# A Fourier mixing layer and a SoLU block: up projection by even and odd parts for tokens k and -k

## The chip, the cores and the metric

The program runs on one core of one Trainium2 chip. The core has five engines that run side by side, each through a queue of its own in order: TensorE (PE, with its weight loads PEld) multiplies matrices into PSUM, VectorE (DVE) and ScalarE (ACT) work on PSUM and SBUF, GpSimd (POOL) works on SBUF, and SyncE (SP) issues transfers; ACT and POOL issue transfers too. The metric is the device time of one execution in microseconds, as the median of several runs.

## The reference

The input x has 8 batches of 3136 tokens with 256 features. A 2D Fourier transform over tokens and features is taken and its real part kept; each of the 25088 tokens then goes through an up projection, a SoLU, a layer norm and a down projection.

```python
X = np.fft.fft(x, axis=1)
X = np.fft.fft(X, axis=2)
x = X.real.reshape(B * S, D)
h = x @ w_in                                   # 256 -> 1024
e = np.exp(h - np.max(h, axis=-1, keepdims=True))
solu = h * e / (np.sum(e, axis=-1, keepdims=True) + 1e-09)
mu = np.mean(solu, axis=-1, keepdims=True)
var = np.mean((solu - mu) ** 2, axis=-1, keepdims=True)
out = (solu - mu) / np.sqrt(var + 1e-06) * g_ln @ w_out   # 1024 -> 256
```

## The kernel before

Everything is float32. A matmul of this type is two instructions in the trace.

**The transform.** A token index is n = 64 n1 + n2, a frequency k = k1 + 49 k2. Batches are taken in 4 pairs. For a pair, x is folded with its mirror x[-n, -d] (`fold`, lines 116 to 128: two sums on POOL, then even and odd parts in the features on DVE), summed over n1 on TensorE (`transform1`, 16 calls a pair, each copied from PSUM by ACT), written to a scratch in HBM and read back with n2 on the partitions (`turn`, 4 transfers on SP). `transform2` then makes, for one k1 of 0 to 24, the 128 tokens of both batches (64 k2 each), as 256 folded features: the cosine part at 0 to 128, the sine part at 129 to 255. The feature transform is folded into w_in before the loop (`Wi`), so that h is the folded features times `Wi`. Token -k has the same cosine part and the sine part negated.

**Two token tiles from one transform2.** DVE copies the PSUM tile to `q` for tokens k (line 169). For tokens -k two ACT steps write `qm`, in reversed order of k2 and with the sine features negated (line 176). From then on k and -k are two separate tiles of 128 tokens: 196 tiles, `+` and `-` in turn (k1 = 0 has no `-`).

**The second part, for one tile.** `up_half` multiplies `q` or `qm` with one half of `Wi` (two calls for the two halves of the features, added in PSUM). `solu`: DVE takes the negated row maximum of h (line 195), ACT the exponential with its sum (198), DVE the product u = h e with its sum (200), POOL the negated mean (203), ACT the centred square with its sum (206), POOL the scale `rs` by four small steps (209 to 215). `transpose` turns u on TensorE in two halves of four; ACT copies the first half to `uT`, DVE the second. `down` is 8 calls with `Wo`, then DVE scales the result into `ot` (237), and SP stores it by two transfers of 64 rows (240).

**The order of the work** is written out by hand (lines 364 to 382) and is the order on every engine: for tile i and the tile before it, the first half of up of i, transposes of i - 1, the second half of up of i, solu of i; after a `+` tile, transform2 for the next k1 and one step of the next pair's sequence transform (`ahead`, 25 steps: loads, 4 folds, 16 transform1, turn); then down of i - 1.

**Buffers that matter.** PSUM has 8 banks: two h tiles of two banks (`ps_h`), two of `tp` (`ps_t`) and two of tag `m` (`ps_m`). The `m` buffers are taken in turn by transform2, transform1 and down. The loads of x use two buffers for each of `xa` and `xb`; xb, the mirrored rows, come by an indirect gather that POOL issues, with row numbers from `idx`.

Before the loop the weights, which come as 64-bit floats, are narrowed on DVE, `Wi` and `Wo` are prepared, and the first pair is transformed.

Of the kernel before, what the change touches and what calls it, by code (L numbers as in the profile page):

```python
# [10 lines left out]
I32 = mybir.dt.int32  # L11
# [6 lines left out]
# The sequence index is n = N2 * n1 + n2 and its frequency k = k1 + N1 * k2.  # L18
# The frequencies k1 of 0..NK-1 are computed; k1 and N1 - k1 share their products.
# [8 lines left out]
# The layout of the 256 folded features: cosine part at 0..128, sine part (1..127) at 129..255.  # L28
# [4 lines left out]
def kernel(  # L33
# [38 lines left out]
    ps_h = ctx.enter_context(tc.tile_pool(name="ps_h", bufs=2, space=PSUM))  # L72
# [9 lines left out]
    neg_half = const.tile([P, 1], FP32, name="neg_half")  # L82
    idx = const.tile([PR, NP * NC], I32, name="idx")
    sg = const.tile([P, 1], FP32, name="sg")

# [8 lines left out]
    def load(pr, c):  # L94
        """Rows n2 = 8c + 1 .. 8c + 8, and those of S - n beside them (in descending order of n2)."""
        r = slice(pr.p * PR, (pr.p + 1) * PR)
        xa = xpool.tile([PR, CH, D], FP32, tag="xa", name="xa")
        xb = xpool.tile([PR, CH, D], FP32, tag="xb", name="xb")
        nc.sync.dma_start(out=xa, in_=x_pn[r, c * CH + 1 : (c + 1) * CH + 1, :])
        i = pr.p * NC + c  # L100
        nc.gpsimd.indirect_dma_start(
            out=xb.rearrange("p l d -> p (l d)"), out_offset=None, in_=x_g,
            in_offset=bass.IndirectOffsetOnAxis(ap=idx[:, i : i + 1], axis=0))
# [12 lines left out]
    def fold(pr, c):  # L116
        """x[n, d] + x[-n, -d], then its even and odd parts in d. Rows n2 = 0 and 32 hold their own mirrors."""
        xa, xb, x0 = pr.raw.pop(c)
# [3 lines left out]
        nc.gpsimd.tensor_tensor(out=a[:, :, 0:1], in0=a[:, :, 0:1], in1=rb[:, :, 0:1], op=ALU.add)  # L122
        y = xpool.tile([PR, CH, D], FP32, tag="y", name="y")
# [31 lines left out]
    def turn(pr):  # L155
        """(b, cosine or sine, n2) onto partitions."""
# [5 lines left out]
    def transform2(pr, k1):  # L162
        """Sum over n2 for both batches; out: folded features on partitions, tokens (b, k2) free."""
        ps = ps_m.tile([P, KD, P], FP32, tag="m", name="ps2")
        for h in range(KD):
            nc.tensor.matmul(ps[:, h, :], pr.g[:, k1, h * P : (h + 1) * P], T[:, k1, :],  # L166
                             start=(h == 0), stop=(h == KD - 1), skip_group_check=True)
        q = {"+": qpool.tile([P, KD, P], FP32, tag="q", name="q")}
        nc.vector.tensor_copy(out=q["+"], in_=ps)  # L169
        if k1:  # L170
            # -(k1 + 49 k2) is (49 - k1) + 49 (63 - k2): the negative frequencies run backwards.
            q["-"] = qpool.tile([P, KD, P], FP32, tag="qm", name="qm")
            for h in range(KD):
                o = q["-"][:, h, :].rearrange("p (b k) -> p b k", b=2)
                i = ps[:, h, :].rearrange("p (b k) -> p b k", b=2)[:, :, ::-1]
                nc.scalar.activation(out=o, in_=i, func=ACT.Copy, scale=sg if h else 1.0)  # L176
        return q

# [1 line left out]

    class Tokens:
        def __init__(self, p, k1, s):
            self.p, self.k1, self.s = p, k1, s

    def up_half(t, half):
        if half == 0:
            t.h = ps_h.tile([P, FF], FP32, tag="h", name="h")
        fs = slice(half * HW, (half + 1) * HW)
        for h in range(KD):
            nc.tensor.matmul(t.h[:, fs], t.q[:, h, :], Wi[:, h, fs], start=(h == 0), stop=(h == KD - 1))  # L190

    def solu(t):
        """u = h exp(h - max h), its sum and centred sum of squares, and the sum of the exponentials."""
        nmax = small.tile([P, 1], FP32, tag="nmax", name="nmax")
        nc.vector.tensor_reduce(out=nmax, in_=t.h, axis=AX.X, op=ALU.max, negate=True)  # L195
        t.u = fpool.tile([P, FF], FP32, tag="u", name="u")
        esum = small.tile([P, 1], FP32, tag="esum", name="esum")
        nc.scalar.activation(out=t.u, in_=t.h, func=ACT.Exp, bias=nmax, accum_out=esum)  # L198
        usum = small.tile([P, 1], FP32, tag="usum", name="usum")
        nc.vector.scalar_tensor_tensor(out=t.u, in0=t.h, scalar=1.0, in1=t.u, op0=ALU.mult, op1=ALU.mult,  # L200
                                       accum_out=usum)
        nmean = small.tile([P, 1], FP32, tag="nmean", name="nmean")
        nc.gpsimd.tensor_scalar(out=nmean, in0=usum, scalar1=-1.0 / FF, scalar2=None, op0=ALU.mult)  # L203
        sq = fpool.tile([P, FF], FP32, tag="sq", name="sq", bufs=1)
        ssq = small.tile([P, 1], FP32, tag="ssq", name="ssq")
        nc.scalar.activation(out=sq, in_=t.u, func=ACT.Square, bias=nmean, accum_out=ssq)  # L206
        # 1 / (sum * sqrt(var(u / sum) + 1e-6)) = (var(u) + 1e-6 sum^2) ** -0.5
        es = small.tile([P, 1], FP32, tag="es", name="es")
        nc.gpsimd.tensor_scalar(out=es, in0=esum, scalar1=1e-9, scalar2=1e-3, op0=ALU.add, op1=ALU.mult)
        es2 = small.tile([P, 1], FP32, tag="es2", name="es2")  # L210
        nc.gpsimd.tensor_tensor(out=es2, in0=es, in1=es, op=ALU.mult)
        v = small.tile([P, 1], FP32, tag="v", name="v")
        nc.gpsimd.tensor_scalar(out=v, in0=ssq, scalar1=1.0 / FF, scalar2=es2, op0=ALU.mult, op1=ALU.add)  # L213
        t.rs = small.tile([P, 1], FP32, tag="rs", name="rs")
        nc.gpsimd.tensor_tensor(out=t.rs, in0=v, in1=neg_half, op=ALU.pow)  # L215

    def transpose(t):
        t.uT = fpool.tile([P, KF, P], FP32, tag="uT", name="uT")
        n = KF // 2
        for half in range(2):  # L220
            tp = ps_t.tile([P, n, P], FP32, tag="t", name="tp")
            for c in range(n):
                f = half * n + c
                nc.tensor.matmul(tp[:, c, :], t.u[:, f * P : (f + 1) * P], ident, is_transpose=True,  # L224
                                 start=(c == 0), stop=(c == n - 1), skip_group_check=True)
            o = t.uT[:, half * n : (half + 1) * n, :]
            if half:
                nc.vector.tensor_copy(out=o, in_=tp)  # L228
            else:
                nc.scalar.copy(o, tp)  # L230

    def down(t):
        ps = ps_m.tile([P, D], FP32, tag="m", name="ps_o")
        for c in range(KF):
            nc.tensor.matmul(ps, t.uT[:, c, :], Wo[:, c, :], start=(c == 0), stop=(c == KF - 1))  # L235
        ot = fpool.tile([P, D], FP32, tag="ot", name="ot", bufs=3)
        nc.vector.tensor_scalar(out=ot, in0=ps, scalar1=t.rs, scalar2=None, op0=ALU.mult)  # L237
        for b in range(2):
            ob = out_b[2 * t.p + b].rearrange("(k2 k1) d -> k1 k2 d", k1=N1)
            nc.sync.dma_start(out=ob[t.k1 if t.s == "+" else N1 - t.k1], in_=ot[b * N2 : (b + 1) * N2, :])  # L240

# [1 line left out]

    def load_weight(pool, w, o, engine):
        """o = w in float32 (rows split as "(c p)"). A float64 w comes as its bits, in words of 32."""
# [11 lines left out]
        def narrow(c, j):  # L257
# [4 lines left out]
            # The exponent, from a bias of 1023 to one of 127.  # L262
# [5 lines left out]
            # top: sign, exponent and the 20 mantissa bits of the high word; unit: the same with no mantissa.  # L268
# [6 lines left out]
            # The low word as a number, by halves that float32 holds exactly.  # L275
# [16 lines left out]
    def load_weights(pool):  # L292
        w_in = pool.tile([P, KD, FF], FP32, name="w_in")
        g_ln = pool.tile([P, KF], FP32, name="g_ln")
        Q = pool.tile([P, KD, D], FP32, name="Q")
# [3 lines left out]
        nc.scalar.dma_start(out=sg, in_=sign)  # L299
# [5 lines left out]
        def prepare():  # L305
            narrow_in()
            for h in range(KD):
                ps = ps_h.tile([P, FF], FP32, tag="h", name="wps")
                for half in range(2):
                    fs = slice(half * HW, (half + 1) * HW)  # L310
                    for c in range(KD):
                        nc.tensor.matmul(ps[:, fs], Q[:, c, h * P : (h + 1) * P], w_in[:, c, fs],
                                         start=(c == 0), stop=(c == KD - 1))
# [137 lines left out]
```

## Time and profile before

| what | us |
| --- | --- |
| median of 3 runs (2170.12 to 2171.92) | 2170.22 |
| span of the profiled execution (first to last instruction) | 2166.9 |
| PE busy in it, 6992 matmul instructions | 1788.7 |
| DVE busy | 846.8 |
| ACT busy | 670.6 |
| POOL busy | 382.0 |

One page sums the whole execution: busy time, share of the span and number of instructions of each engine. Other views cut it: windows give the busy time of each engine in a stretch, with the clock that TensorE was granted (1.00 is full speed) and the DMA share; waits say which engine and line waited for which, with the total, the number of times and the longest; groups (`line engine op out<-in shapes xcount | busy, mean ns | idle before`) give a mean duration; a timeline gives start, duration, engine, line and step, with the idle time before it and what ended that in brackets. PE and PEld durations of neighbouring instructions overlap, so the price of a TensorE step is read from start to start. The loop over the tiles begins at 136.6 us.

### The profile page before, as it was taken

What the parts mean: (1) busy time and instruction counts of PE and PEld (TensorE: products, weight loads), DVE (VectorE), ACT (ScalarE), POOL (GpSimd) and SP (SyncE); (2) the same over time, 40 slices, a digit from 0 to 9 for tenths busy, and PEclk for the clock granted to TensorE, in tenths of its full rate; (3) what the DMA queues carried; (4) which work ended last, traced back from release to release, by engine and by line L of the source; (5) the groups of instructions that cost most, each with busy time, mean ns of one, the idle gap of its engine ahead of it and who ended that gap; (6) DMA issues with size and microseconds to landing.
All of it is one profiled execution on the core that took longest, in us unless ns stands there. A gap on an engine that the chain in (4) does not pass through costs nothing. (4 is left out here: it accounts for less than half of the span.)

```text
span 2166.9 us, 19414 instructions
## 1 busy us (share of the span) xinstructions
PE 1788.7 (83%) x6992; PEld 1238.2 (57%) x6992; DVE 846.8 (39%) x1327; ACT 670.6 (31%) x1240; POOL 382.0 (18%) x1034
## 2 busy tenths in 40 slices
PE   2357888788799878878879987887887999999998
PEld 1135555555566555555556755555555666777666
DVE  2853233323334323332433433333233344444444
ACT  1113223223333322332332323233233234434443
POOL 3002121212112212121211221212121111111111
PEclk8679899889899888888999988889899899999999
DMA  9511010001042101000104210101010400000000
GB/s 240 133 33 42 24 46 13 25 13 28 10 90 75 42 20 50 12 26 12 28 11 88 77 42 16 54 10 28 11 29 11 88 18 18 17 16 18 18 18 17
DMA packets 56783, 84.78 MB, mean 39 GB/s; under 512 B 12038, under 2 KB 50574, under 8 KB 51696
## 3 DMA queue, kind: packets, MB, share of 16 engines
q1 hardware_dynamic: 48528, 65.19, 12.7%
q0 software_dynamic: 2048, 12.85, 2.1%
q10 hardware_dynamic: 6112, 5.52, 1.3%
q8 instruction: 55, 0.90, 0.2%
q14 instruction: 40, 0.33, 0.1%
HBM read 44.72 MB, written 38.80 MB: 39 GB/s over the span
## 5 line engine op out<-in xcount | busy, mean ns | idle before, releaser
L235 PE MATMUL ps_o<-Wo,uT 128*128 128x256 f32 x3136 | 833.5, 425 | 270.8 <-ACT qm L176 215.9
L235 PEld LDWEIGHTS ps_o<-Wo,uT 128*128 128x128 f32 x3136 | 668.7, 217 | 444.7 <-ACT qm L176 235.5
L198 ACT ACTIVATE u<-h,nmax 128x1024 f32<-128x1024 f32 x196 | 218.4, 1114 | 634.3 <-DVE nmax L195 634.3
L190 PE MATMUL h<-Wi,q 128*128 128x512 f32 x800 | 384.4, 604 | 7.8 <-DVE q L169 7.8
L190 PE MATMUL h<-Wi,qm 128*128 128x512 f32 x768 | 361.1, 592 | 0.0
L200 DVE SCALAR_TENSOR_TENSOR u<-h,u 128x1024 f32<-128x1024 f32 x196 | 240.0, 1225 | 249.4 <-ACT u L198 249.4
L206 ACT ACTIVATE sq<-u,nmean 128x1024 f32<-128x1024 f32 x196 | 225.1, 1148 | 317.7 <-POOL nmean L203 317.7
L195 DVE TENSOR_REDUCE nmax<-h 128x1 f32<-128x1024 f32 x196 | 239.9, 1224 | 193.5 <-PE h L190 193.5
L203 POOL TENSOR_SCALAR nmean<-usum 128x1 f32<-128x1 f32 x196 | 45.7, 233 | 1515.3 <-DVE u L200 1515.3
L228 DVE COPY uT<-tp 128x512 f32<-128x512 f32 x196 | 135.5, 691 | 372.3 <-PE tp L224 372.3
L230 ACT COPY uT<-tp 128x512 f32<-128x512 f32 x196 | 114.9, 586 | 415.9 <-PE tp L224 415.9
L224 PEld LDWEIGHTS tp<-ident,u 128*128 128x128 f32 x1568 | 183.5, 141 | 104.5 <-issue 103.7
L237 DVE TENSOR_SCALAR ot<-ps_o,rs 128x256 f32<-128x256 f32 x196 | 94.0, 480 | 369.4 <-issue 364.3
L190 PEld LDWEIGHTS h<-Wi,q 128*128 128x128 f32 x800 | 147.5, 195 | 115.4 <-issue 103.7
L224 PE MATMUL tp<-ident,u 128*128 128x128 f32 x1568 | 203.2, 273 | 0.5 <-DVE u L200 0.5
L190 PEld LDWEIGHTS h<-Wi,qm 128*128 128x128 f32 x768 | 138.4, 190 | 96.8 <-issue 91.8
L215 POOL TENSOR_TENSOR rs<-v,neg_half 128x1 f32<-128x1 f32 x196 | 113.2, 578 | 16.3
L148 PE MATMUL ps<-y,F 98*100 98x258 f32 (+3 forms) x288 | 71.5, 385 | 43.3 <-DVE y L114 43.3
L166 PEld LDWEIGHTS ps<-T,g 128*128 128x128 f32 x400 | 60.4, 191 | 47.4 <-issue 47.4
L213 POOL TENSOR_SCALAR v<-ssq,es 128x1 f32<-128x1 f32 x196 | 52.4, 267 | 177.6 <-ACT sq L206 175.5
L148 PEld LDWEIGHTS ps<-y,F 98*100 98x100 f32 x288 | 45.5, 178 | 54.7 <-DVE y L114 30.4
L121 POOL TENSOR_TENSOR xa<-xa,xb 98x2040 f32<-98x2040 f32 (+1 forms) x16 | 70.1, 4379 | 28.9 <-DMA xa<-in_x_dram 16.2
(50 smaller groups left out, 544.4 us busy)
## 6 DMA issues: line engine op xcount, KB each, us to landing
out_dram<-ot SPq DMA_DIRECT2D x392, 64.0 KB
zd<-z SPq DMA_DIRECT2D x16, 800.0 KB
g<-zd SPq DMA_DIRECT2D x16, 800.0 KB
xa<-in_x_dram SPq DMA_DIRECT2D x16, 784.0 KB
raw_in_moe_w_in_dram<-in_moe_w_in_dram ACTq DMA_DIRECT2D x1, 2048.0 KB
raw_in_moe_w_out_dram<-in_moe_w_out_dram ACTq DMA_DIRECT2D x1, 2048.0 KB
T<-in_t_tab_dram ACTq DMA_DIRECT2D x2, 400.0 KB
x<-in_x_dram SPq DMA_DIRECT2D x4, 98.0 KB
```

The costliest lines, as they stand in the source:

```text
L148: nc.tensor.matmul(o[..., cs], F[:, 2 * t + h, :], i[..., cs], start=first, stop=True, skip_group_check=True)
L190: nc.tensor.matmul(t.h[:, fs], t.q[:, h, :], Wi[:, h, fs], start=(h == 0), stop=(h == KD - 1))
L195: nc.vector.tensor_reduce(out=nmax, in_=t.h, axis=AX.X, op=ALU.max, negate=True)
L198: nc.scalar.activation(out=t.u, in_=t.h, func=ACT.Exp, bias=nmax, accum_out=esum)
L200: nc.vector.scalar_tensor_tensor(out=t.u, in0=t.h, scalar=1.0, in1=t.u, op0=ALU.mult, op1=ALU.mult, accum_out=usum)
L206: nc.scalar.activation(out=sq, in_=t.u, func=ACT.Square, bias=nmean, accum_out=ssq)
L215: nc.gpsimd.tensor_tensor(out=t.rs, in0=v, in1=neg_half, op=ALU.pow)
L224: nc.tensor.matmul(tp[:, c, :], t.u[:, f * P : (f + 1) * P], ident, is_transpose=True, start=(c == 0), stop=(c == n - 1), skip_group_check ...
L228: nc.vector.tensor_copy(out=o, in_=tp)
L230: nc.scalar.copy(o, tp)
L235: nc.tensor.matmul(ps, t.uT[:, c, :], Wo[:, c, :], start=(c == 0), stop=(c == KF - 1))
L237: nc.vector.tensor_scalar(out=ot, in0=ps, scalar1=t.rs, scalar2=None, op0=ALU.mult)
```

## The change

Tokens k and -k of one k1 become one unit. Its up projection is made once for the cosine features (0 to 127, `up(t, 0)`) and once for the sine features (128 to 255, `up(t, 1)`) in two PSUM tiles. Feature 128, a cosine one, goes out of the second part: its column of `Wi` is kept apart as a row `w_mid`, the feature itself is brought onto token partitions by a further matmul with one column in transform2, and DVE adds it while it takes the even part from PSUM (`even`). DVE then makes h for k as even + odd and for -k as even - odd, with the row maximum in the same instruction (`join`); the maxima are negated by one small step. The `qm` copies go.

The tokens of -k are now in the order of k, so their rows in the output run backwards: they are stored by an indirect scatter that POOL issues (`idx` has a column for each). h now lies in SBUF; the square is written over it.

The order of steps is written anew for units, and the loop's fold is split: the sums on POOL (`add_mirror`) come one step before the DVE part (`fold`), and `ahead_pe` (transform1, turn) stands apart from `ahead` (load, add_mirror, fold). The four small steps for `rs` are made for both signs at once, in five.

```diff
-    ps_h = ctx.enter_context(tc.tile_pool(name="ps_h", bufs=2, space=PSUM))
+    ps_h = ctx.enter_context(tc.tile_pool(name="ps_h", bufs=1, space=PSUM))
...
-    idx = const.tile([PR, NP * NC], I32, name="idx")
-    sg = const.tile([P, 1], FP32, name="sg")
+    idx = const.tile([P, NP * (NC + NK - 1)], I32, name="idx")
+    w_mid = const.tile([P, FF], FP32, name="w_mid")
...
     def transform2(pr, k1):
-        ps = ps_m.tile([P, KD, P], FP32, tag="m", name="ps2")
+        ps = ps_m.tile([P, KD * P + 1], FP32, tag="m", name="ps2")
...
+        nc.tensor.matmul(ps[:, KD * P :], T[:, k1, :], pr.g[:, k1, P : P + 1],
+                         start=False, stop=True, skip_group_check=True)
+        return ps
+
+    def take2(ps):
+        q = qpool.tile([P, KD * P + 1], FP32, tag="q", name="q")
+        nc.vector.tensor_copy(out=q, in_=ps)
         return q
...
-    def up_half(t, half):
-        if half == 0:
-            t.h = ps_h.tile([P, FF], FP32, tag="h", name="h")
-        fs = slice(half * HW, (half + 1) * HW)
-        for h in range(KD):
-            nc.tensor.matmul(t.h[:, fs], t.q[:, h, :], Wi[:, h, fs], start=(h == 0), stop=(h == KD - 1))
+    def up(t, c):
+        ps = ps_h.tile([P, FF], FP32, tag=f"h{c}", name=f"ps_h{c}")
+        for half in range(2):
+            fs = slice(half * HW, (half + 1) * HW)
+            nc.tensor.matmul(ps[:, fs], t.q[:, c * P : (c + 1) * P], Wi[:, c, fs], start=True, stop=True)
+        return ps
+
+    def even(t, ps):
+        t.ev = fpool.tile([P, FF], FP32, tag="ev", name="ev", bufs=1)
+        nc.vector.scalar_tensor_tensor(out=t.ev, in0=w_mid, scalar=t.q[:, KD * P :], in1=ps,
+                                       op0=ALU.mult, op1=ALU.add)
+
+    def join(t, ps):
+        t.nmax = small.tile([P, 2], FP32, tag="nmax", name="nmax")
+        for s in t.signs:
+            t.h[s] = fpool.tile([P, FF], FP32, tag="h", name="h", bufs=2)
+            nc.vector.tensor_tensor_reduce(out=t.h[s], in0=t.ev, in1=ps, scale=1.0, scalar=-3.0e38,
+                                           op0=ALU.subtract if s else ALU.add, op1=ALU.max,
+                                           accum_out=t.nmax[:, s : s + 1])
+        n = len(t.signs)
+        t.neg = small.tile([P, 2], FP32, tag="neg", name="neg")
+        nc.vector.tensor_scalar(out=t.neg[:, 0:n], in0=t.nmax[:, 0:n], scalar1=-1.0, scalar2=None, op0=ALU.mult)
...
+    def store(t, s, ps):
+        ot = fpool.tile([P, D], FP32, tag="ot", name="ot", bufs=4)
+        nc.vector.tensor_scalar(out=ot, in0=ps, scalar1=t.rs[:, s : s + 1], scalar2=None, op0=ALU.mult)
+        if s:
+            i = NP * NC + t.p * (NK - 1) + t.k1 - 1
+            nc.gpsimd.indirect_dma_start(
+                out=out, out_offset=bass.IndirectOffsetOnAxis(ap=idx[:, i : i + 1], axis=0), in_=ot, in_offset=None)
+            return
...
+        if r == 4 and c + 1 < NC:
+            add_mirror(pr, c + 1)
         elif 0 <= c < NC and r == 0:
             fold(pr, c)
...
+            if cur:
+                even(cur, up(cur, 0))
+            if prv:
+                uT = transpose(prv, 0)
+            if cur:
+                odd = up(cur, 1)
+            if prv:
+                ps0 = down(prv, uT)
+            if cur:
+                join(cur, odd)
+                expo(cur)
+                product(cur, 0)
+            if prv:
+                store(prv, 0, ps0)
+            if two:
+                uT = transpose(prv, 1)
+            if nxt:
+                nxt.q = take2(transform2(pairs[nxt.p], nxt.k1))
+            if cur:
+                square(cur, 0)
+                if cur.p + 1 < NP:
+                    ahead_pe(pairs[cur.p + 1], cur.k1)
+            if two:
+                ps1 = down(prv, uT)
+            if cur:
+                if 1 in cur.signs:
+                    product(cur, 1)
+                    square(cur, 1)
+                stats(cur)
+                if cur.p + 1 < NP:
+                    ahead(pairs[cur.p + 1], cur.k1)
+            if two:
+                store(prv, 1, ps1)
```

`expo`, `product`, `square` and `stats` are the steps of `solu` for one sign (the last for both); `cur` is the unit at hand, `prv` the one before it, `nxt` the one after, and `two` says that `prv` has both signs. In the loop that prepares the weights a third product makes `w_mid`.

More of the change, by code (lines that the diff above doesn't have):

```diff
@@ new lines, in expo, with product @@
+    def expo(t):
+        t.esum = small.tile([P, 2], FP32, tag="esum", name="esum")
+        for s in t.signs:
+            t.u[s] = fpool.tile([P, FF], FP32, tag="u", name="u", bufs=4)
+            nc.scalar.activation(out=t.u[s], in_=t.h[s], func=ACT.Exp, bias=t.neg[:, s : s + 1],
+                                 accum_out=t.esum[:, s : s + 1])
+    def product(t, s):
+        if s == 0:
+            t.usum = small.tile([P, 2], FP32, tag="usum", name="usum")
+            t.nmean = small.tile([P, 2], FP32, tag="nmean", name="nmean")
+        nc.vector.scalar_tensor_tensor(out=t.u[s], in0=t.h[s], scalar=1.0, in1=t.u[s], op0=ALU.mult,
+                                       op1=ALU.mult, accum_out=t.usum[:, s : s + 1])
+        nc.gpsimd.tensor_scalar(out=t.nmean[:, s : s + 1], in0=t.usum[:, s : s + 1], scalar1=-1.0 / FF,
+                                scalar2=None, op0=ALU.mult)
@@ new lines, in square, with stats @@
+    def square(t, s):
+        if s == 0:
+            t.ssq = small.tile([P, 2], FP32, tag="ssq", name="ssq")
+        nc.scalar.activation(out=t.h[s], in_=t.u[s], func=ACT.Square, bias=t.nmean[:, s : s + 1],
+                             accum_out=t.ssq[:, s : s + 1])
+    def stats(t):
+        n = slice(0, len(t.signs))
+        es = small.tile([P, 2], FP32, tag="es", name="es")
+        nc.gpsimd.tensor_scalar(out=es[:, n], in0=t.esum[:, n], scalar1=1e-9, scalar2=1e-3,
+                                op0=ALU.add, op1=ALU.mult)
+        es2 = small.tile([P, 2], FP32, tag="es2", name="es2")
+        nc.gpsimd.tensor_tensor(out=es2[:, n], in0=es[:, n], in1=es[:, n], op=ALU.mult)
+        v = small.tile([P, 2], FP32, tag="v", name="v")
+        nc.gpsimd.tensor_scalar(out=v[:, n], in0=t.ssq[:, n], scalar1=1.0 / FF, scalar2=None, op0=ALU.mult)
+        nc.gpsimd.tensor_tensor(out=v[:, n], in0=v[:, n], in1=es2[:, n], op=ALU.add)
+        t.rs = small.tile([P, 2], FP32, tag="rs", name="rs")
+        nc.gpsimd.tensor_tensor(out=t.rs[:, n], in0=v[:, n], in1=neg_half[:, n], op=ALU.pow)
@@ L219, in transpose @@
+    def transpose(t, s):
+        uT = fpool.tile([P, KF, P], FP32, tag="uT", name="uT", bufs=2)
         n = KF // 2
@@ L367 @@
+        units[0].q = take2(transform2(pairs[0], 0))
+        for i in range(len(units) + 1):
+            cur = units[i] if i < len(units) else None
+            nxt = units[i + 1] if i + 1 < len(units) else None
+            prv = units[i - 1] if i else None
+            two = prv is not None and 1 in prv.signs
             if cur:
-                cur.q = qs[cur.p, cur.k1][cur.s]
-                up_half(cur, 0)
+                even(cur, up(cur, 0))
             if prv:
-                transpose(prv)
+                uT = transpose(prv, 0)
```

115 lines of the change are left out of this document (42 added, 73 removed).

## The prediction

> **What bounds the kernel now.** I read the busy time of the engines first, then windows over the span, then the waits.
>
> ```profile
> PE 1788.7 (83%) x6992; PEld 1238.2 (57%) x6992; DVE 846.8 (39%) x1327; ACT 670.6 (31%) x1240; POOL 382.0 (18%) x1034
> 900.00:1080.00 180.00, 144.06 (x544) 100.41 (x545) 62.20 (x93) 52.72 (x99) 30.72 (x79) 0.89 0.08 20
> 1900.00:2160.00 260.00, 258.63 (x1104) 181.81 (x1103) 120.77 (x179) 105.44 (x195) 48.30 (x165) 1.00 0.08 17
> PE ps_o L235 <- ACT qm L176: 215.9, 48, 4.5
> PE ps_o L235 <- DVE uT L228: 54.0, 12, 4.5
> ```
>
> In the windows (after the length: PE, PEld, DVE, ACT, POOL busy, then the clock) the last pair of batches keeps TensorE busy for 258.63 of 260 us at clock 1.00: TensorE bounds it. The earlier pairs also transform the next pair's sequence, and there TensorE is busy for 144 of 180 us at clock 0.89. The waits say why: 48 stalls behind `qm` (3 pairs x 16 calls of transform1) and 12 behind `uT` (3 x 4 folds), 4.5 us each. No other engine is busy for half the span.
>
> The timeline of the last pair gives the price of each step, from start to start:
>
> ```profile
> 1953.38 0.61 PE L166 MATMUL ps<-T,g 128*128 128x128 f32 x4
> 1953.82 3.62 PE L235 MATMUL ps_o<-Wo,uT 128*128 128x256 f32 x16
> 1957.22 0.42 DVE L169 COPY q<-ps 128x256 f32<-128x256 f32 x1
> 1957.28 1.88 PE L190 MATMUL h<-Wi,qm 128*128 128x512 f32 x4
> 1957.56 0.48 DVE L237 TENSOR_SCALAR ot<-ps_o,rs 128x256 f32<-128x256 f32 x1
> 1957.66 1.15 ACT L206 ACTIVATE sq<-u,nmean 128x1024 f32<-128x1024 f32 x1 [1.62 <-POOL nmean L203]
> 1958.99 1.04 PE L224 MATMUL tp<-ident,u 128*128 128x128 f32 x8
> 1959.63 0.59 ACT L230 COPY uT<-tp 128x512 f32<-128x512 f32 x1 [0.30 <-PE tp L224]
> 1959.87 1.88 PE L190 MATMUL h<-Wi,qm 128*128 128x512 f32 x4
> 1960.07 0.69 DVE L228 COPY uT<-tp 128x512 f32<-128x512 f32 x1 [2.03 <-PE tp L224]
> 1961.58 3.62 PE L235 MATMUL ps_o<-Wo,uT 128*128 128x256 f32 x16
> 1961.79 1.23 DVE L195 TENSOR_REDUCE nmax<-h 128x1 f32<-128x1024 f32 x1 [1.03 <-PE h L190]
> 1963.05 1.11 ACT L198 ACTIVATE u<-h,nmax 128x1024 f32<-128x1024 f32 x1 [2.83 <-DVE nmax L195]
> 1964.06 0.19 ACT L198 ACTIVATION_READ_ACCUMULATOR u<-h,nmax 128x1 f32 x1
> 1964.28 1.23 DVE L200 SCALAR_TENSOR_TENSOR u<-h,u 128x1024 f32<-128x1024 f32 x1 [1.27 <-ACT u L198]
> 1965.04 1.88 PE L190 MATMUL h<-Wi,q 128*128 128x512 f32 x4
> 1965.43 0.48 DVE L237 TENSOR_SCALAR ot<-ps_o,rs 128x256 f32<-128x256 f32 x1
> ```
>
> On TensorE: four up matmuls 1.71 (1957.28 to 1958.99), a transpose of eight 0.88, a down projection 3.46, transform2 0.44. A token tile is 2 x 1.71 + 0.88 + 3.46 = 7.76, a unit (k and -k) 15.96. Across engines: DVE sees a finished PSUM tile 0.21 after the next matmul begins (1961.58, 1961.79), a transposed half 0.2 after its matmuls; DVE to ACT takes 0.03; exp to product 1.23. Back to back, DVE begins the next step 0.08 before the last has ended (1957.22, 1957.56).
>
> **The stalls go.**
>
> ```profile
> 189.47 1.03 PE L148 MATMUL ps<-y,F 98*100 98x258 f32 x4
> 194.62 0.36 ACT L176 ACTIVATE qm<-ps,sg 128x128 f32<-128x128 f32 x1
> 195.03 5.41 PE L235 MATMUL ps_o<-Wo,uT 128*128 128x256 f32 x16 [4.53 <-ACT qm L176]
> 200.27 1.88 PE L190 MATMUL h<-Wi,qm 128*128 128x512 f32 x4
> ```
>
> transform1 takes the second `m` buffer, so the down projection waits for the buffer that `qm` still reads, and `qm` stands behind the squares on ACT. It then runs its 16 matmuls in 5.24 instead of 3.46: a half clock follows the idle time. A stall costs 4.5 + 1.8 = 6.3 us or more. Of the loop's 2026 us (136.62 to 2162.6), 96 x 15.96 + 4 x 8.20 + 48 x 0.86 = 1606 are TensorE's work, so some 410 us are stalls. `qm` is removed, and add_mirror moves a step ahead of its fold, so that no fold holds DVE.
>
> **The work that goes and comes.** For a unit of two signs, four up matmuls of 1.71 become two: -3.42 us, 328 us over 96 units. The column for 128 adds two matmuls of one column with their weight loads; not shown; between 0.05 and 0.44 (a whole transform2), I take 0.22 by the 0.11 of each of its four. TensorE's unit is then 12.76, or 13.62 with transform1 (0.86).
>
> DVE gains `even` (1.23; its two inputs, PSUM and SBUF, are those of L200) and `neg` (nearest row below: 0.16). The joins take the place of the maximum, 1.23 each by L195 and L200, which also has an accumulator. No row shows this step: `uT`'s 512 columns and the maximum's 1024 lie 0.54 us apart, so between 1.08, with no fixed part, and 2.3, at half that rate. The exps read SBUF as the square does (1.15 against 1.11), 7 us in all, left to the range. DVE's sum is 9.2 us a unit, so it isn't the bound, but its chain now is. With t = 0 at the unit's first up matmul:
>
> - TensorE: up 0 to 1.71, transpose to 2.59, up to 4.30, down to 7.76, transpose to 8.64, transform2 to 9.30; it is ready for the second down then.
> - DVE: even 1.92 to 3.15, `uT` to 3.76, join 4.51, join 5.66 to 6.89, neg to 7.06.
> - ACT: exp 7.09, second exp 8.19, then only `uT` of the second sign, 9.29 to 9.88: its queue is in order.
> - DVE: product 8.32, `ot` 9.47 to 9.95 (it frees the buffer of the second down), `uT` to 10.56, transform2's copy to 10.90, second product to 12.05.
>
> So the second down begins at 9.99 in place of 9.30, and with 0.1 for a restart the unit ends at 13.55. With transform1, its matmuls wait for that same `ot`, run from 9.99 to 10.85, the down waits for the copy at 10.90, and the unit takes 14.44. These waits stand at the head of TensorE's queue: the next unit's up waits with them. Of single signs, three units end at 12.8 (one join, one exp) and four at 10.4 (no second down, but the next up needs the copy).
>
> What stands beside this, at nothing:
>
> ```profile
> L121 POOL TENSOR_TENSOR xa<-xa,xb 98x2040 f32<-98x2040 f32 x12 | 54.2, 4514 | 25.7 <-DMA xa<-in_x_dram 13.0 <-DMA xb<-in_x_dram,idx 12.7
> L101 POOL DMA_INDIRECT xb<-in_x_dram,idx x16 | 21.9, 1368 | 7.2 <-DMA idx<-in_mirror_dram 2.8 <-POOL xa L122 2.5 <-issue 1.8
> L215 POOL TENSOR_TENSOR rs<-v,neg_half 128x1 f32<-128x1 f32 x196 | 113.2, 578 | 16.3
> L112 DVE TENSOR_TENSOR y<-xa 98x1016 f32<-98x1016 f32 x16 | 19.5, 1218 | 122.2 <-POOL xa L121 122.2
> L281 DVE SCALAR_TENSOR_TENSOR rest<-ex,rest 128x256 f32<-128x256 int32 x8 | 3.4, 425 | 0.3
> L283 DVE TENSOR_TENSOR rest<-rest,unit 128x256 f32<-128x256 f32 x8 | 3.4, 425 | 0.3
> L114 DVE COPY y<-x 98x2 f32<-98x2 f32 x4 | 0.6, 160 | 0.0
> DMA to landing us min/median/max: 6.2/7.7/20.3
> 624.25 3.77 SPq L159 DMA_DIRECT2D g<-zd  x4
> 645.00:650.00 5.00, 5.00 (x25) 3.71 (x24) 1.86 (x4) 2.84 (x5) 1.03 (x5) 1.00 0.07 16
> ```
>
> POOL: two nmean, five small steps (0.2 to 0.58) and a scatter are 3.3 of 13.55 us. No row shows a scatter: between 0.58, a step that moves nothing, and 20.3, if POOL waited for the worst landing (last row but two, the gathers' landings); I take 1.37, the gather's own row. add_mirror (4.7) runs from about 15 to 5.2 of the next unit, the scatter behind it to 6.6, before nmean is due at 9.6. fold's 2.9 us follow the second product, end near 14.8, and `ot` and even come just in time. SP loses a quarter of its stores. turn has nearly three units, 38 us, of cover; its transfers, issued from 624, had ended by 645 (DMA share 0.07), 21 us. ACT loses `qm`. With the cover of add_mirror gone, 12 x 4.7 = 56 us.
>
> **The sum.**
>
> ```profile
> 136.62 5.37 PE L190 MATMUL h<-Wi,q 128*128 128x512 f32 x8 [3.26 <-DVE q L169]
> 146.20 1.98 PE L190 MATMUL h<-Wi,q 128*128 128x512 f32 x4 [3.77 <-DVE q L169]
> 2162.66 0.48 DVE L237 TENSOR_SCALAR ot<-ps_o,rs 128x256 f32<-128x256 f32 x1 [4.00 <-PE ps_o L235]
> ```
>
> The loop begins at 136.6, and 1.0 later with the third weight product and the larger index table. First iteration 9.8 (136.62 to 146.20, and neg). Then 44 x 13.55 + 48 x 14.44 + 3 x 12.8 + 4 x 10.4 = 1369. Tail 16: two transposes and downs, 10, then `ot`, the scatter and its landing, where the plain store needed 3.7 (2163.1 to the span's end). 137.6 + 9.8 + 1369 + 16 = 1532 us of span. The median before lies 3.3 above the profiled span (2170.2, 2166.9): **1536 us**.
>
> **Rivals.**
>
> *The product at half rate.* It now reads `h` and `u` both from SBUF, with an accumulator. The two SBUF inputs of L281 cost 425 ns for 256, as much as L283's plain product, so two inputs alone cost nothing; the accumulator with them no row shows. At half rate `ot` and all behind it come 1.08 later, 92 x 1.08 = 99: 1635 us. "Vector Engine (DVE) Microarchitecture Reference" of the Trainium skill, section "Points that are easy to get wrong", says just this of such a step with two float32 SBUF inputs; by it the time is 1635, by L281's row 1536.
>
> *The joins at half rate:* 2 x 1.07 a unit, 92 x 2.14 = 197: 1733.
>
> *Order on the output.* Were scatter and plain stores kept in order because both write `out`, a store would wait for a landing (7.7 by the gather, hidden; 20.3 at worst). In the 12 units with add_mirror the scatter lands near 14.3, some 5 late, and under three turns 10: 12 x 5 + 3 x 10 = 90, 1626.
>
> *The clock.*
>
> ```profile
> 687.84 1.98 PE L190 MATMUL h<-Wi,q 128*128 128x512 f32 x4 [0.26 <-DVE q L169]
> ```
>
> 0.26 us of idle time left the four matmuls near full speed, 4.5 did not; 0.7 lies between, nearer the first. If each unit lost the stall's 1.8 to 3.5, 92 x 2.6 = 240: about 1775.
>
> *Slower than before: POOL becomes the bound.* If a scatter held POOL until it had landed, the unit would be the scatter plus 1.9. Slower needs (2167 - 164 - 80) / 92 = 20.9 a unit, a scatter over 19 us: the worst landing, 20.3, as the rule, gives 137.6 + 26 + 80 + 92 x 22.2 = 2286. The 1.37 row speaks against it.
>
> *The change doesn't do what it says:* the ring of two `m` buffers jams as before, 48 x 6.3 = 302: 1838.
>
> **Chances.** Forecast 0.66 (itself 1500 to 1590: from half the waits gone, 92 x 0.4, to 0.6 more in each unit), product 0.10, joins 0.06, order 0.08, clock 0.05, jam 0.03, POOL 0.02. Range 1500 to 1680: it takes in the forecast, the product and the order, 0.84. Faster by over 0.2% (what a measurement here can tell from no change) 0.97, within 0.01, slower 0.02.
>
> **What would show it.** Right: up matmuls of L190's kind fall from 1568 to 800; TensorE's idle time sits before the second down, 0.7 us, behind `uT` on ACT, `ot` or the copy; no 4.5 us stalls; clock 1.00 from the loop's start; units of 13.6 and 14.4. Wrong: a product or join over 1.3 us, POOL waiting on stores, or a clock under 1.00 in steady state.

## The result and the profile after

The changed kernel takes 1575.9 us (median, 1574.95 to 1576.94) against 2170.2 before: a ratio of 0.7258, with a 95% interval of 0.7247 to 0.7268. The profiled execution has a span of 1573.4 us, 2.5 below the median.

First the page's line of busy times:

```profile
PE 1372.6 (87%) x6432; PEld 1043.2 (66%) x6432; DVE 965.8 (61%) x1725; ACT 621.2 (39%) x1049; POOL 413.0 (26%) x846
```

Then two of its windows (as before: length, then PE, PEld, DVE, ACT and POOL busy, the clock, the DMA share, GB/s):

```profile
900.00:1080.00 180.00, 169.27 (x811) 129.42 (x810) 111.47 (x193) 81.23 (x139) 51.04 (x104) 1.00 0.13 38
...
1300.00:1550.00 250.00, 233.30 (x1118) 180.91 (x1119) 156.55 (x273) 107.52 (x182) 54.87 (x144) 1.00 0.07 20
```

And the two largest waits of TensorE behind `ot` (total, times, longest), with the row of the weight loads that belong to the first of them (PEld; `...` stands for lines left out, here and below):

```profile
PE ps_o L276 <- DVE ot L282: 42.7, 43, 2.2
...
PE ps L152 <- DVE ot L282: 38.9, 48, 0.8
...
PEld ps_o L276 <- ACT uT L270: 47.7, 46, 2.3
```

The stretch with the next pair's transform has TensorE busy for 169 of 180 us where it was 144, at clock 1.00 where it was 0.89. The 60 stalls of 4.5 us are gone. What is left is a wait of 0.8 or 0.9 us in nearly every unit of two signs (2.2 us in three of them), behind `ot`: 48 times ahead of transform1 and 43 times ahead of the second down projection. The last pair, which was bound by TensorE, no longer is: 233 of 250.

The timeline of one unit of the last pair shows the chain that the prediction laid out; a line has start, duration, engine and line, and in brackets the idle time ahead of it and what ended that. The unit begins at 1400.13 with its first up projection:

```profile
1400.13 1.88 PE L198 MATMUL ps_h<-Wi,q 128*128 128x512 f32 x4
...
1404.44 3.62 PE L276 MATMUL ps_o<-Wo,uT 128*128 128x256 f32 x16
...
1404.74 1.22 DVE L212 CUSTOM_DVE_ANT_0 h<-ev,ps_h 128x1024 f32<-128x1024 f32 x1 [0.81 <-PE ps_h L198]
...
1405.89 1.22 DVE L212 CUSTOM_DVE_ANT_0 h<-ev,ps_h 128x1024 f32<-128x1024 f32 x1
...
1407.14 0.17 DVE L217 TENSOR_SCALAR neg<-nmax 128x2 f32<-128x2 f32 x1
1407.35 1.15 ACT L223 ACTIVATE u<-h,neg 128x1024 f32<-128x1024 f32 x1 [4.28 <-DVE neg L217]
...
1408.62 1.23 DVE L231 SCALAR_TENSOR_TENSOR u<-h,u 128x1024 f32<-128x1024 f32 x1 [1.31 <-ACT u L223]
...
1409.63 0.56 ACT L270 COPY uT<-tp 128x512 f32<-128x512 f32 x1
...
1409.78 0.48 DVE L282 TENSOR_SCALAR ot<-ps_o,rs 128x256 f32<-128x256 f32 x1
...
1410.40 3.69 PE L276 MATMUL ps_o<-Wo,uT 128*128 128x256 f32 x16 [0.90 <-DVE ot L282]
...
1413.93 1.88 PE L198 MATMUL ps_h<-Wi,q 128*128 128x512 f32 x4
```

Join, join, neg, exp, product, `ot`: the second down begins 10.27 after the unit, 0.9 after TensorE was ready, and the unit takes 13.80. The ACT copy of `uT` ends at 1410.19 and `ot` at 1410.26: two chains that end within 0.07 us. TensorE's row of the wait names `ot`, the row of its weight loads names `uT`.

### The profile page after: what moved, and what is told of

Its sections match the earlier page's. It is cut to its first block, busy times and chain, and to the rows that moved or that the text cites. A ratio compares the mean times of both kernels' runs of the same rounds, so it can differ in the third digit from the quotient of the medians.

```text
span 1573.4 us, 17844 instructions
## 1 busy us (share of the span) xinstructions
PE 1372.6 (87%) x6432; PEld 1043.2 (66%) x6432; DVE 965.8 (61%) x1725; ACT 621.2 (39%) x1049; POOL 413.0 (26%) x846
## 4 chain that ended last, share of the span: by engine, by line
PE 56%; DVE 24%; issue 9%; ACT 8%; DMA 2%; DVEq 1%; POOL 1%; POOLq 0%; SPq 0%; ACTq 0%
PE ps_o L276 24%; PE ps_h L198 22%; DVE h L212 14%; ACT u L223 7%; PE tp L264 6%; PE ps L152 4%; DVE ot L282 2%; DVE ex L303 1%; DVE neg L217 1%; DMA xa<-in_x_dram 1%; DMA xb<-in_x_dram,idx 1%; DVE u L231 1%; POOL xa L121 1%; DVE rest L331 0%; DVE rest L333 0%
## 5 line engine op out<-in xcount | busy, mean ns | idle before, releaser
L276 PE MATMUL ps_o<-Wo,uT 128*128 128x256 f32 x3136 | 721.1, 383 | 44.7 <-DVE ot L282 42.7
L276 PEld LDWEIGHTS ps_o<-Wo,uT 128*128 128x128 f32 x3136 | 591.3, 191 | 181.5 <-issue 61.4
L223 ACT ACTIVATE u<-h,neg 128x1024 f32<-128x1024 f32 x196 | 223.6, 1142 | 434.3 <-DVE neg L217 434.3
L198 PE MATMUL ps_h<-Wi,q 128*128 128x512 f32 x800 | 379.2, 597 | 14.7 <-DVE q L180 14.7
L231 DVE SCALAR_TENSOR_TENSOR u<-h,u 128x1024 f32<-128x1024 f32 x196 | 239.2, 1220 | 130.9 <-ACT u L223 130.9
L212 DVE CUSTOM_DVE_ANT_0 h<-ev,ps_h 128x1024 f32<-128x1024 f32 x196 | 231.7, 1219 | 81.6 <-PE ps_h L198 81.6
L240 ACT ACTIVATE h<-u,nmean 128x1024 f32<-128x1024 f32 x196 | 225.1, 1148 | 101.6 <-POOL nmean L233 99.0
L198 PEld LDWEIGHTS ps_h<-Wi,q 128*128 128x128 f32 x800 | 144.6, 191 | 117.5 <-issue 100.7
L204 DVE SCALAR_TENSOR_TENSOR ev<-w_mid,q,ps_h 128x1024 f32<-128x1024 f32 x100 | 128.1, 1281 | 119.8 <-PE ps_h L198 119.8
L285 POOL DMA_INDIRECT out_dram<-ot,idx x96 | 102.9, 1072 | 71.1 <-DVE ot L282 41.8
L255 POOL TENSOR_TENSOR rs<-v,neg_half 128x2 f32<-128x2 f32 (+1 forms) x100 | 71.8, 718 | 7.8
```

Source lines behind the costliest of these rows:

```text
L198: nc.tensor.matmul(ps[:, fs], t.q[:, c * P : (c + 1) * P], Wi[:, c, fs], start=True, stop=True)
L204: nc.vector.scalar_tensor_tensor(out=t.ev, in0=w_mid, scalar=t.q[:, KD * P :], in1=ps, op0=ALU.mult, op1=ALU.add)
L212: nc.vector.tensor_tensor_reduce(out=t.h[s], in0=t.ev, in1=ps, scale=1.0, scalar=-3.0e38, op0=ALU.subtract if s else ALU.add, op1=ALU.max, ...
L223: nc.scalar.activation(out=t.u[s], in_=t.h[s], func=ACT.Exp, bias=t.neg[:, s : s + 1], accum_out=t.esum[:, s : s + 1])
L231: nc.vector.scalar_tensor_tensor(out=t.u[s], in0=t.h[s], scalar=1.0, in1=t.u[s], op0=ALU.mult, op1=ALU.mult, accum_out=t.usum[:, s : s + 1])
L240: nc.scalar.activation(out=t.h[s], in_=t.u[s], func=ACT.Square, bias=t.nmean[:, s : s + 1], accum_out=t.ssq[:, s : s + 1])
```

## The experiments

Before them stood two things to settle: how much of the gain is order and how much is work, and whether the wait that is left is the chain that the prediction named. Three theories were tried: the old stalls are the ring of two `m` buffers and the fold's place in DVE's queue; TensorE's removed work counts in full; the second down waits for two chains at once.

### The old kernel with the down projection ahead

```diff
                 solu(cur)
+            if prv:
+                down(prv)
+            if cur:
                 if cur.s == "+":
...
                         ahead(pairs[cur.p + 1], cur.k1)
-            if prv:
-                down(prv)
```

> The kernel before, with the down projection of the tile before issued ahead of transform2 and transform1 instead of behind them. Theory (the 48 stalls are the ring of two m buffers, held by the qm copies): they go with the half clock behind them, and a wait of about 0.5 us for ot stays in front of transform1: 2170 - 48 x 6.4 = about 1860 us; the 12 stalls at the folds stay. Rival (the stalls belong to transform1's own chain and only change their place): above 2100 us.

Measured: 1864.1 us, ratio 0.8587 (0.8573 to 0.8601). The waits of TensorE in it:

```profile
PE ps_o L235 <- DVE uT L228: 49.2, 12, 4.1
...
PE ps L148 <- DVE ot L237: 15.4, 48, 0.3
```

The 48 stalls behind `qm` became 48 waits of 0.3 us in front of transform1, and 306 us went with them. The idle time itself is 216 us (48 x 4.5) less the 15 of the new waits. Most of the rest is the slow stretch behind each stall: the 48 down projections took 5.60 us on average in the old kernel (5.00 to 5.85) where an undisturbed one takes 3.46, which makes 48 x 2.1 = 103 us; the mean granted clock of the run rises from 0.90 to 0.96.

### The same, and the sums on POOL a step ahead of the fold

```diff
-        elif 0 <= c < NC and r == 0:
+        if r == 4 and c + 1 < NC:
+            add_mirror(pr, c + 1)
+        if 0 <= c < NC and r == 0:
             fold(pr, c)
...
```

The lines left out split `fold` into `add_mirror` and `fold`.

> The kernel before, with the down projection ahead as in the run before this one and the sums on POOL a step ahead of the DVE part of the fold. Theory (DVE waits in its queue for POOL, and uT behind it): another 12 x 6.5 = 78 us less, about 1780 us. Rival (the 2.9 us of the fold on DVE hold uT up by themselves): within 10 us of the run before. What is left from here to the changed kernel is then the price of the halved up projection less the new waits.

Measured: 1791.4 us, ratio 0.8258 (0.8243 to 0.8273), 73 below the run before it. No wait of a down for `uT` on DVE is left. So in the old kernel order alone, with no instruction of the second part changed, is worth 2170 - 1791 = 379 us, where the whole gain of the change is 594.

### The new kernel with the old amount of up work

```diff
-        for half in range(2):
+        for half in (0, 1, 0, 1):
```

> The changed kernel with each up matmul issued twice into the same place (the second overwrites the first with the same values), so that TensorE has the up work of the kernel before. Theory (the chain behind the second up sets when the second down begins, so all of the added work passes into the time): 100 x 3.42 = 342 us more, 1918 us. Rival (TensorE's idle 0.9 us in each unit takes up part of it): 262 us more, 1838 us or less.

Measured: 1916.6 us, 340.7 above the changed kernel. Units go from 13.80 to 17.23 and from 14.73 to 18.16: the added 3.43 pass through whole, although TensorE idles for 0.9 us in each unit. The idle time stands behind the second up (join, exp, product, `ot`), so a longer up moves it rather than filling it. Read the other way, the halved up projection is worth its full price.

If the two may be added, the account is 379 for the order and 341 for the up work against 594 measured. The 126 us between them, which the new structure gives back, are a remainder and not measured as such; a run below finds 98 us of waits.

### The sums on POOL beside their fold again

```diff
-        if r == 4 and c + 1 < NC:
-            add_mirror(pr, c + 1)
         elif 0 <= c < NC and r == 0:
+            add_mirror(pr, c)
             fold(pr, c)
```

> The changed kernel with the sums on POOL back in the step of their fold. By the prediction's price (12 x 4.7 us): 1576 + 56 = 1632 us. Rival (the wait holds ot and even too, and the half clock follows, as in the kernel before): 12 x 7 to 9 us, 1660 to 1685 us. Second rival (the new order has room for it): within 10 us of 1576.

Measured: 1637.7 us, ratio 0.7548 (0.7535 to 0.7560), 62 above. TensorE's new wait in it:

```profile
PE ps_o L276 <- DVE uT L268: 51.9, 12, 4.4
```

The unit behind a fold takes 20.5 to 20.8 instead of 14.73, about 5.9 more and not 4.7: TensorE idles for 4.3 us there, not 0.8, and the matmuls behind it run slowly (eight of a down in 3.58 us where they take 1.73). But the three units behind a k1 = 1 fall from 16.9 to 13.9, for a reason found below. 12 x 5.9 - 3 x 3 = 62. The price of 56 was near by luck: two errors of opposite sign.

### ot first, uT first, both

In the first of these, `store(prv, 0, ps0)` stands ahead of `product(cur, 0)`. In the second, the first half of the second sign's transposes, with its ACT copy, stands ahead of the second exp:

```diff
-                expo(cur)
-                product(cur, 0)
+                expo(cur, (0,))
+            if two:
+                uT1 = fpool.tile([P, KF, P], FP32, tag="uT", name="uT", bufs=2)
+                turn_half(prv, 1, uT1, 0)()
+            if cur:
+                expo(cur, cur.signs[1:])
             if prv:
                 store(prv, 0, ps0)
+            if cur:
+                product(cur, 0)
             if two:
-                uT = transpose(prv, 1)
+                last = turn_half(prv, 1, uT1, 1)
+                last()
...
```

(This is both; each alone leaves the other's lines where they were. `turn_half` issues four of the transposes and returns their copy to `uT`, which is issued when it is called.)

> The changed kernel with ot of the first sign on DVE ahead of the product of the unit at hand. Theory (the second down waits for two chains that end within 0.1 us of each other, ot on DVE and uT behind two exps on ACT): units without transform1 stay within 0.1 us of 13.80; units with it, whose transform1 waits for ot alone, gain 0.2 to 0.5 us: 10 to 25 us less, 1551 to 1566. Rival (ot alone is the wait, as the profile names it): all 92 units gain 0.8 us, about 1500.

> The changed kernel with the first half of uT of the second sign on ACT ahead of the second exp. Theory (two chains): ot still holds the second down, within 8 us of 1576. Rival (uT on ACT alone is the wait): 44 units gain 0.8 us, about 1540.

> The changed kernel with both moves. Theory (two chains): units without transform1 fall from 13.80 to 12.9 (TensorE's own work), those with it to about 14.4, where the second down waits for the copy of transform2: 44 x 0.9 + 48 x 0.35 = 56 us less, about 1520, more than the two moves add up to alone. Rival (a third wait is just behind them): under 30 us less.

Measured: `ot` first 1549.8 us (ratio 0.7133, 0.7123 to 0.7143); `uT` first 1575.5 (0.7257, 0.7243 to 0.7272); both 1504.1 (0.6924, 0.6914 to 0.6934). The moves alone give 26 and 0 us, together 72. TensorE's waits, `ot` first:

```profile
PE ps_o L276 <- ACT uT L270: 37.8, 46, 2.1
...
PE ps_o L276 <- DVE q L180: 22.5, 45, 0.8
```

and `uT` first, where the row names an exp 34 times (`ot` in nine more):

```profile
PE ps_o L280 <- ACT u L224: 30.7, 34, 0.9
...
PE ps L152 <- DVE ot L286: 38.9, 48, 0.8
```

With `ot` out of the way, the same second down waits for `uT` on ACT, and units without transform1 go from 13.80 only to 13.66; those with it go from 14.73 to 14.33, where the copy of transform2 is the last wait (the second row). With `uT` out of the way, they stay at 13.80, and the profile puts the wait down to the exp of the second sign. That exp isn't what holds it, as the timeline of this run shows:

```profile
1411.47 1.15 ACT L224 ACTIVATE u<-h,neg 128x1024 f32<-128x1024 f32 x1
...
1412.23 0.48 DVE L286 TENSOR_SCALAR ot<-ps_o,rs 128x256 f32<-128x256 f32 x1
...
1412.52 0.19 ACT L224 ACTIVATION_READ_ACCUMULATOR u<-h,neg 128x1 f32 x1
...
1412.86 3.48 PE L280 MATMUL ps_o<-Wo,uT 128*128 128x256 f32 x15 [0.90 <-ACT u L224]
```

The exp's accumulator read and `ot` both end at 1412.71; the row took the one, the buffer waited for the other. The run with both moves shows it, in a unit of the last pair (its first up, its second down, the next unit's first up):

```profile
1340.19 1.88 PE L198 MATMUL ps_h<-Wi,q 128*128 128x512 f32 x4
...
1349.42 3.70 PE L280 MATMUL ps_o<-Wo,uT 128*128 128x256 f32 x16
...
1352.95 1.88 PE L198 MATMUL ps_h<-Wi,q 128*128 128x512 f32 x4
```

The second exp's accumulator read ends at 1350.31 there, 10.12 behind the unit's start as in the run with `uT` first, and the second down begins 0.89 before that end. The unit takes 12.76. The theory of two chains holds, and "behind `ot`" in the profile after was half of the truth.

### The copy of transform2 first too

```diff
-                uT = transpose(prv, 1)
+                last = turn_half(prv, 1, uT1, 1)
             if nxt:
                 nxt.q = take2(transform2(pairs[nxt.p], nxt.k1))
+            if two:
+                last()
```

> The changed kernel with both moves, and the copy of transform2 on DVE ahead of the second half of uT. Theory (in the units with transform1 the copy is the last wait): they fall to about 13.8, 12.8 of work and 1.0 for transform1: 44 x 0.9 + 48 x 0.9 = 83 us less, about 1493, and TensorE is the bound. Rival (uT's second half is late then): no better than the run before.

Measured: 1477.9 us, ratio 0.6808 (0.6798 to 0.6817). The windows of it (columns as above):

```profile
300.00:450.00 150.00, 150.00 (x728) 115.31 (x727) 101.03 (x176) 69.12 (x118) 43.57 (x92) 1.00 0.19 47
1300.00:1450.00 150.00, 150.00 (x727) 116.22 (x726) 101.02 (x176) 68.37 (x116) 36.32 (x95) 1.00 0.07 21
```

TensorE has no idle time left in either stretch: 12.76 for a unit and 13.74 with transform1. The waits that the new structure brought were worth 1575.9 - 1477.9 = 98 us, and none of them was necessary.

### Negating the maxima by another instruction

Three units, each behind a k1 = 1, took 16.87 to 16.89, where the fourth of this kind, in the last pair and with no POOL sum, took 13.89. In the changed kernel's timeline of the second of them (POOL, DVE and TensorE):

```profile
520.80 4.50 POOL L121 TENSOR_TENSOR xa<-xa,xb 98x2040 f32<-98x2040 f32 x1
...
523.88 1.46 DVE L217 TENSOR_SCALAR neg<-nmax 128x2 f32<-128x2 f32 x1
...
528.42 5.38 PE L276 MATMUL ps_o<-Wo,uT 128*128 128x256 f32 x16 [2.19 <-DVE ot L282]
```

The negation of 128 x 2 values took 1.46 us instead of 0.17 and ended, at 525.34, when the POOL sum ended, at 525.30. Everything behind it came 1.29 later, the down waited for 2.19, and its 16 matmuls then ran in 5.22 instead of 3.53. The unit for k1 = 1 is short (10.41 here), so the sum begins late in the unit behind it; the other nine sums of the loop end 2.1 to 2.6 us ahead of the next negation.

```diff
-        nc.vector.tensor_scalar(out=t.neg[:, 0:n], in0=t.nmax[:, 0:n], scalar1=-1.0, scalar2=None, op0=ALU.mult)
+        nc.vector.tensor_reduce(out=t.neg[:, 0:n], in_=t.nmax[:, 0:n].rearrange("p (s o) -> p s o", o=1),
+                                axis=AX.X, op=ALU.max, negate=True)
```

> The changed kernel with the maxima negated by a reduction over one element instead of a tensor_scalar step. In the three units after a k1 = 1 the tensor_scalar took 1.45 us instead of 0.17 and ended when the POOL sums of add_mirror ended. Theory (a float32 tensor_scalar from SBUF to SBUF and a POOL step that reads SBUF exclude each other, as the Trainium skill's SBUF page says of a two-port mode, which a reduction does not have): the reduction takes 0.2 us there too, the three units fall from 16.9 by 1.3 and by the 1.8 of half clock behind their 2.2 us of idle time: about 9 us less, 1567. Rival (DVE waits for something else, or any DVE step of SBUF operands is held): the step still takes over 1 us in those units and the time stays.

Measured: 1566.5 us, ratio 0.7212 (0.7202 to 0.7222), 9.5 below the changed kernel. The group of the negation (count, busy time, mean ns, idle time ahead):

```profile
L217 DVE TENSOR_REDUCE neg<-nmax 128x2 f32<-128x2 f32 x96 | 14.9, 155 | 3.3
```

And the same place in its timeline:

```profile
521.37 4.51 POOL L121 TENSOR_TENSOR xa<-xa,xb 98x2040 f32<-98x2040 f32 x1
...
524.45 0.15 DVE L217 TENSOR_REDUCE neg<-nmax 128x2 f32<-128x2 f32 x1
...
527.70 3.69 PE L277 MATMUL ps_o<-Wo,uT 128*128 128x256 f32 x16 [0.90 <-DVE ot L283]
```

The reduction runs in the midst of the POOL sum and takes 0.15, in this place as in all others (153 to 156 ns). The first two of the three units take 13.89. The third takes 15.56, for another reason, ahead of its negation (its first up and the transposes behind it):

```profile
872.78 2.46 PE L198 MATMUL ps_h<-Wi,q 128*128 128x512 f32 x4 [1.91 <-DVE q L180]
875.03 1.91 PE L265 MATMUL tp<-ident,u 128*128 128x128 f32 x8
```

These take 2.25 and 1.70, where the unit at 516.76 of the changed kernel, behind 1.92 us of idle time, takes 1.83 and 0.87. The profile is of the longest of five runs (1564.78 to 1570.51). Three units at 13.89 would be 3 x 3.0 = 9 us less, which is what the median shows.

### Plain stores in place of the scatter

In `store`, the tokens of -k take the two plain transfers as well, to the rows of 49 - k1. This kernel leaves out the reversal of their order, so that those rows of its output are not the reference's; the bytes stored are as many.

> The changed kernel with the tokens of -k stored by two plain transfers on SP in place of the scatter on POOL; their rows are left in the order of k, so those rows of the output are not the reference's. Theory (the scatter is 1.07 us on a POOL that is idle for most of a unit, and only the last one shows): within 4 us of 1576, the last store aside. Rival (POOL's queue, held by scatters that wait for ot, delays nmean and the squares): 20 us less or more.

Measured: 1569.2 us, ratio 0.7222 (0.7211 to 0.7234), 6.7 below the changed kernel. Its units take the same 13.80 and 14.73. From the last `ot` to the end of the span are 3.7 us (1564.1 to 1567.8) against 11.2 with the scatter (1562.2 to 1573.4). So the scatter shows only at the very end.

### All moves together

> All three moves of order and the negation by a reduction. Theory: the three units after a k1 = 1 lose their last wait of 0.9 us and the rest is TensorE's own work: about 3 us less than without the reduction, 1475. Rival: the same time as without it, 1478.

Measured: 1470.6 us, ratio 0.6777 (0.6766 to 0.6789) to the kernel before, 105 below the changed kernel, and 7 below the run without the reduction. The reduction took 1.1 us from each of the three units (13.94 to 12.86), 3.3 in all, and the two profiled spans differ by as much (1475.8, 1472.4). The other 4 us between the medians stay open; the runs spread over 5 (1470.18 to 1475.44), and the profile is of one near the upper end (1474.49).

## Why the prediction came out as it did

It forecast 1536 us within 1500 to 1680; measured are 1575.9, 40 above, 2.6%. By its own sum, against the span of 1573.4:

| term | predicted | measured |
| --- | --- | --- |
| start of the loop | 137.6 | 136.0 |
| first iteration | 9.8 | 9.8 |
| 44 units without transform1 | 44 x 13.55 = 596 | 40 x 13.80, 3 x 16.88, 13.89 = 616 |
| 48 units with transform1 | 48 x 14.44 = 693 | 45 x 14.73, 3 x 15.03 = 708 |
| 3 iterations into a k1 = 0 | 38 | 38.5 |
| 4 iterations out of one | 42 | 43.4 |
| tail | 16 | 21.5 |

- **The stalls go.** Right in the cause: order alone took 379 us from the old kernel in two steps. The prediction's 410 is a slip (2026 - 1606 is 420; the forecast does not use it), and a stall cost more than its 6.3, 4.5 + 2.1. The other 41 of the 420 stayed in the old kernel, and no run tells where.
- **Up work.** Right: 3.42 a unit predicted, 3.43 in the run that put it back.
- **The chain.** Right: the second down does wait for `ot` and `uT`, and the predicted 9.99 came at 10.27. The steps mis-sized are small ones: DVE began the join 0.30 after the next matmul, not 0.21 (1404.44 to 1404.74), which with rounding makes 0.10; negation and exp came 0.03 later still (7.22 behind the unit's start, not 7.09), `ot` began 0.05 more behind that exp, and the down began 0.14 after `ot` ended, not 0.04. The restart, taken at 0.1, was 0.07. That is the 0.25 in a unit without transform1.
- **transform1** was taken at 0.86, with 0.05 for the copy behind it; behind a wait it takes 1.02 (199.80 to 200.82 in one unit) and the copy is no longer the last wait. It began 0.19 later than predicted by the chain above (10.18 in place of 9.99), so the units came to 14.73, 0.29 more than forecast. The last unit of a pair that has one, with its extra parts, took 15.03. The two rows of units are 35 us above the forecast: 10 and 15 by these two points, 10 by the next.
- **"What stands beside this, at nothing".** This is the part that failed. add_mirror was placed by the length of a normal unit, to end 5.2 into the next one (4.9 measured), ahead of the negation at 6.9; behind the short unit of k1 = 1 it ends at 8.5, overlaps the negation and holds it: 3 x 3.1 = 9 us. The prediction had looked for queues that it is late in, and not for an engine that it can hold.
- **Tail.** Of the 16, about 6 were for `ot`, the scatter and its landing; from the end of the last `ot` alone it is 11.2. The last scatter lands 2.4 us after its issue at 1562.4, so its landing is not what is long. Behind it, no engine works and no transfer moves until the span ends (length, the five engines' busy time, clock, DMA share, GB/s):

```profile
1566.00:1568.00 2.00, 0.00 (x0) 0.00 (x0) 0.00 (x0) 0.00 (x0) 0.00 (x0) 0.50 0.00 0
1568.00:1570.00 2.00, 0.00 (x0) 0.00 (x0) 0.00 (x0) 0.00 (x0) 0.00 (x0) 0.50 0.00 0
1570.00:1573.40 3.40, 0.00 (x0) 0.00 (x0) 0.00 (x0) 0.00 (x0) 0.00 (x0) 0.50 0.00 0
```

With plain stores alone the end is 3.7. What the program waits for in these 7 us is not shown.

The 41 us between the summed span (1532) and the measured one are thus no single error but several small ones, nearly all of one sign: 10 and 15 in the two kinds of units, 10 by add_mirror, 6 in the tail.

The rivals, first in the changed kernel's groups:

```profile
L231 DVE SCALAR_TENSOR_TENSOR u<-h,u 128x1024 f32<-128x1024 f32 x196 | 239.2, 1220 | 130.9 <-ACT u L223 130.9
L212 DVE CUSTOM_DVE_ANT_0 h<-ev,ps_h 128x1024 f32<-128x1024 f32 x196 | 231.7, 1219 | 81.6 <-PE ps_h L198 81.6
...
L285 POOL DMA_INDIRECT out_dram<-ot,idx x96 | 102.9, 1072 | 71.1 <-DVE ot L282 41.8 <-issue 9.6 <-DVE u L231 8.5
```

and in the waits of its SP queue:

```profile
SPq L290 <- DMA out_dram<-ot,idx: 702.5, 92, 15.7
```

- *Product and joins at half rate* fall by the first two rows: 1220 and 1219 ns. "Vector Engine (DVE) Microarchitecture Reference" of the Trainium skill, "Points that are easy to get wrong", has the product at half rate with two float32 SBUF inputs; here the trace doesn't agree: the same step with one input in PSUM took 1225 ns before.
- *Order on the output* was a true mechanism with no price. The plain stores wait for the scatters 92 times, 702 us in all, by the last row; no unit is longer for it, as the run with plain stores, in which no such wait is left, shows (its units are the same).
- *The clock* stayed at 1.00 through idle times of 0.9 us in every unit.
- *POOL as the bound* and *the jam* did not happen: a scatter takes 1.07 us of POOL, and no stall of 4.5 us is left.

## What to carry to other kernels

Look for the stalls before the work: here two changes of the order of issue were worth more (379 us, in the old kernel) than halving the up projection (341). Where a wait joins two chains that end together, moving either gives little (26 and 0 us here) and moving both gives far more than the sum (72). The name in the profile's row is only the one that ended last by a hair, and once here it was a bystander that ended in the same hundredth of a microsecond. When a long POOL step is moved, ask not only what it is late for but also which DVE steps it overlaps.

## What the runs showed of the hardware

- A DVE tensor_scalar from SBUF to SBUF in float32, of two elements a partition, took up to 1.47 us beside a POOL sum, against 0.17 alone; a reduction in the same place took 0.15. "SBUF — State Buffer" of the Trainium skill, section "Who interferes with whom", says that such a step can take a port pair which DVE and GpSimd hold only in turn, and that a reduction never contends; the trace agrees with both.
- The other way round: POOL's small steps stretch beside the DVE sums of the fold, which read two SBUF tensors. In the changed kernel:

```profile
530.27 1.21 DVE L112 TENSOR_TENSOR y<-xa 98x1016 f32<-98x1016 f32 x1
...
530.43 1.11 POOL L233 TENSOR_SCALAR nmean<-usum 128x1 f32<-128x1 f32 x1 [2.23 <-DVE u L231]
```

1.11 us for a step of 0.23, ending within 0.1 us of the sum. The square on ACT waits for it, but no time was lost here: the unit behind takes 14.73 like the others.
- Idle times of 0.9 us every 13.8 us never lowered the granted clock (1.00 in both windows of the profile after). Those of 1.9 us were followed by matmuls at full speed four times in the changed kernel and at about half speed once in four in the run with the reduction (2.25 us in place of 1.8, then 1.70 in place of 0.87); the three of 2.2 us by a down of 5.2 us in place of 3.5 each time, and the 48 of 4.1 to 4.5 us behind `qm` in the kernel before by one of 5.0 to 5.85 us, where 3.46 is usual.
- The two matmuls of one column, with their weight loads, cost 0.14 us where TensorE is the bound (in the run with the copy first, 1412.38 to 1412.52), 0.07 each. One of 128 columns in the same transform2 costs 0.11, so a single column is far from free.
